# Attention and mixture: the mixture's products as single float32 matmuls instead of three rounded ones

## The chip, the cores and the metric

The kernel runs on one core of a Trainium2 chip. The metric is the device time of one execution in microseconds, and the median of the runs counts. Engines are named as in the profile: PE multiplies matrices (PEld is its loading of weights), DVE, ACT and POOL work element by element, SP issues transfers.

## What is computed

Eight batches, each of eight attention heads (576 positions, 64 wide), followed by a mixture over the joined heads (512 channels):

```python
scores = scale * np.matmul(q, k.transpose(0, 1, 3, 2))
thresh = np.max(scores, axis=-1, keepdims=True) - tau
scores = np.where(scores >= thresh, scores, -1000000000.0)
...
attn = attn / (np.sum(attn, axis=-1, keepdims=True) + 1e-09)
return np.matmul(attn, v).astype(np.float32)
...
theta = x @ w_theta
cos_t, sin_t = (np.cos(theta), np.sin(theta))
zr = x * cos_t
zi = x * sin_t
yr = np.einsum('ts,bsd->btd', w_tok_r, zr)
yi = np.einsum('ts,bsd->btd', w_tok_i, zi)
y = yr + yi
u = x + y
return (u + np.maximum(u @ w_ch, 0.0)).astype(np.float32)
```

The weights come as float64, and the kernel converts them to float32 on the chip.

## The kernel before, in words

Everything is transposed: a tile xT holds 128 channels by 576 positions. Heads go in pairs, four pairs to a batch, 32 in all. A pair has five blocks of query rows, worked off as nine "halves". One half is: scores on PE (line 278), their eviction with the row minimum on DVE (L282), exp on ACT (L299), mask and row sum on DVE (L300), transposes on PE (L326, L341) copied by ACT (L331, L344). After the second block and at the end of a pair come the values (o_ps, L361, copied to xT by L362) and the division by the row sums (normalize).

The mixture of a batch runs beside the attention of the next one. It is a generator, `moe`, that yields a cost after each piece of PE work. `fill` is called twice in each half; it adds `share` to an account and takes pieces of the mixture until the account is used up. The order of PE's instructions is the order in which the program issues them (`manual_schedule`); the other engines' order comes from priorities, where attention goes first. Attention's scores run three halves ahead (`AHEAD`). The last batch's mixture has no attention beside it.

The mixture has three stages with matmuls, in the order of `ORDER`:

- angle: th = w_theta times x, for four blocks m of 128 channels, two halves of 288 positions, four blocks to sum over (`product`, L405). th is evicted by ACT (m under 2) or DVE (L446), reduced to a fraction of a turn on DVE (km, L453, and L454, L463), and ACT takes sine and cosine (L471, L472). POOL multiplies them by x (L483), DVE in the last batch.
- token: z is transposed on PE in nine blocks (L495), evicted, and multiplied by the token weights, nine blocks to sum over (L512). The sum is added to xT in place (L515), which makes it u.
- channel: w_ch times u (`product` again), evicted with the maximum and added to u in place (L560), and u goes out by DMA (L565).

A product of two float32 matrices is made of three matmuls on rounded halves: high times high, low times high, high times low. So every operand is split: `split` copies it to a rounded type (float32r) for the high half and subtracts that for the low half. x is split when the batch's attention is done (split_x: ACT and POOL, the last chunk on DVE); z when it is evicted (zh on ACT, L497, zl on DVE, L498); u after the token stage (split_u: DVE and POOL). The token weights stay in SBUF as wt_h and wt_l. The halves of w_theta and w_ch are written to DRAM (wm_dram), and for each m POOL's queue loads them again (get_wm, L192).

The conversion of the weights is spread over the first halves: `fill` advances one of two streams at each call (`load_weight`; bit operations on ACT and DVE, L138 to L148). For w_theta and w_tok the two float32 parts are added on PE through the identity (w_ps, L159 and L160); for w_ch, which comes later, on DVE (L150).

Of the kernel before, what the change touches and what calls it, by code (L numbers as in the profile page):

```python
# [16 lines left out]
DRAM = bass.MemoryType.DRAM  # L17
# [16 lines left out]
LAG = 3  # L34
# [5 lines left out]
def tile_attn_moe(  # L40
# [22 lines left out]
    dram = ctx.enter_context(tc.tile_pool(name="dram", bufs=1, space=DRAM))  # L63
# [56 lines left out]
    turn = [0]  # L120

    def load_weight(src, n, on_pe=True):

        w = pool.tile([P, S], F32, tag="xh", name="w", bufs=4)[:, :n]
        if src.dtype == F32:
            nc.sync.dma_start(w, src)
            yield
            return [(slice(0, n), w)]
        turn[0] += 1
        tag, bufs = ("wm", 3) if turn[0] % 2 else ("z", 3)  # L130
        raw = pool.tile([P, S, 2], U32, tag=tag, name="wraw", bufs=bufs)[:, :n]
        nc.sync.dma_start(raw, src.bitcast(U32).rearrange("p (n t) -> p n t", t=2))
        low, high = raw[:, :, 0], raw[:, :, 1]
        bits = pool.tile([P, S], U32, tag="xh", name="bits", bufs=4)[:, :n]
        mag = pool.tile([P, S], U32, tag="xl", name="mag", bufs=4)[:, :n]
# [11 lines left out]
        nc.vector.tensor_scalar(out=mag, in0=bits, scalar1=0xFF800000, scalar2=None, op0=ALU.bitwise_and)  # L147
        nc.vector.scalar_tensor_tensor(out=w, in0=low, scalar=2.0**-52, in1=magf, op0=ALU.mult, op1=ALU.mult)  # L148
        if not on_pe:
            nc.vector.tensor_tensor(out=w, in0=w, in1=bitsf, op=ALU.add)  # L150
            yield
            return [(slice(0, n), w)]
        yield

        n2 = n if n <= 512 else n // 2
        got = []
        for c in range(0, n, n2):
            ps = ps_t.tile([P, 512], F32, tag="t", name="w_ps")[:, :n2]
            nc.tensor.matmul(ps, ident, bitsf[:, c : c + n2], start=True, stop=False)  # L159
            nc.tensor.matmul(ps, ident, w[:, c : c + n2], start=False, stop=True)  # L160
            got.append((slice(c, c + n2), ps))
        return got

    def load_wtok(c):
        got = yield from load_weight(w_tok[c * P : (c + 1) * P, :], S)
        for r, w in got:
            split(nc.scalar, nc.vector, wt_h[:, c, r], wt_l[:, c, r], w)

    def load_wm(which, src, c):
        got = yield from load_weight(src[c * P : (c + 1) * P, :], DM, which == 0)  # L170
        hi, lo = (pool.tile([P, DM], F32R, tag="zh4" if x == "whi" else "zl4", name=x, bufs=4) for x in ("whi", "wlo"))
        for r, w in got:
            split(nc.scalar, nc.vector, hi[:, r], lo[:, r], w)
        for i, t in enumerate((hi, lo)):
            nc.sync.dma_start(
                wm_dram[which, :, :, i, c, :].rearrange("m p e -> p m e"),
                t.bitcast(F32).rearrange("p (m e) -> p m e", e=P),
            )
# [10 lines left out]

    def get_wm(which, m):  # L190
        t = pool.tile([P, 2, NM, P], F32R, tag="wm", name=f"wm{which}", bufs=3)
        nc.gpsimd.dma_start(t, wm_dram[which, m].bitcast(F32R))  # L192
        return t
# [156 lines left out]
    def values(pr, g):  # L350
# [3 lines left out]
        if pr.n not in xT:  # L354
            xT[pr.n] = pool.tile([P, S], F32, tag="xT", name=f"xT{pr.n}", bufs=7)
# [33 lines left out]
    def product(wm, parts, todo, together):  # L389

        terms = ((0, 0), (1, 0), (0, 1))
        if together:

            runs = [[(h, *t, c) for t in terms[:2] for c in range(NM - 1)] for h in range(2)]
            runs += [[(h, *terms[2], c) for c in range(NM - 1)] for h in range(2)]
            runs += [[(h, *t, NM - 1) for t in terms] for h in range(2)]
        else:
            runs = [[(h, *t, c) for t in terms for c in range(NM)] for h in range(2)]
        tiles, count = {}, [0, 0]
        for run in runs:  # L400
            for n, (h, a, bb, c) in enumerate(run):
# [3 lines left out]
                nc.tensor.matmul(  # L405
                    tiles[h][:, :HS], wm[:, a, c, :], parts[c][bb][:, hs], start=(count[h] == 0), stop=(count[h] == 11)
                )
                count[h] += 1
                if count[h] == 12:
# [4 lines left out]
    def halves(which):  # L414
        hi = pool.tile([P, S], F32R, tag="xh", name=which + "h", bufs=4)
        lo = pool.tile([P, S], F32R, tag="xl", name=which + "l", bufs=4)
        return hi, lo

    parts = {}

    def split_x(b):
        parts[b] = []
        for c in range(NM):
            hi, lo = halves("x")
            split(nc.vector if c == NM - 1 else nc.scalar, nc.vector if c == NM - 1 else nc.gpsimd, hi, lo, xT[b * NP + c])
            parts[b].append((hi, lo))

    def moe(b):
        last = b == B - 1


        lo_eng = nc.vector if last else nc.gpsimd

        xs = parts.pop(b)
        zs = {}

        def angle(m):
            th = temp("th")
            wm = get_wm(0, m)
# [10 lines left out]
            yield from product(wm, xs, evict, m == 0)  # L450
# [6 lines left out]
        def sines(ms):  # L457

            todo = []
            for m in ms:  # L460
                th = zs.pop((m, "f"))
                z = pool.tile([P, 2 * S], F32, tag="z", name="z", bufs=3)
# [16 lines left out]
            for m, th, z in todo:  # L479
                x = xT[b * NP + m]  # L480
# [5 lines left out]
        def flip(m):  # L486
            z = zs.pop(m)
            out = []
            for c0, nb in ((0, 4), (4, 1), (5, 4)):
                zh = pool.tile([P, nb, P], F32R, tag=f"zh{nb}", name="zh", bufs=4 if nb == 4 else 2)  # L490
                zl = pool.tile([P, nb, P], F32R, tag=f"zl{nb}", name="zl", bufs=4 if nb == 4 else 2)
# [4 lines left out]
                tv = tp[:, : nb * P].rearrange("p (c q) -> p c q", q=P)  # L496
                nc.scalar.copy(out=zh, in_=tv)  # L497
                nc.vector.tensor_tensor(out=zl, in0=tv, in1=zh.bitcast(F32), op=ALU.subtract)  # L498
                out += [(zh[:, i], zl[:, i]) for i in range(nb)]
                yield 110 * nb  # L500
            zs[m, "T"] = out

        def token(m):
            zz = zs.pop((m, "T"))
            x = xT[b * NP + m]
            for h in range(2):
                hs = slice(h * HS, (h + 1) * HS)
                ps = ps_t.tile([P, 512], F32, tag="t", name="y_ps")
                work = [(zz[c][0], w[:, c, hs]) for c in range(NK) for w in (wt_h, wt_l)]
                work += [(zz[c][1], wt_h[:, c, hs]) for c in range(NK)]  # L510
                for n, (z, w) in enumerate(work):
                    nc.tensor.matmul(ps[:, :HS], z, w, start=(n == 0), stop=(n == len(work) - 1))  # L512
                    if n % 3 == 2:
                        yield 393
                nc.vector.tensor_tensor(out=x[:, hs], in0=ps[:, :HS], in1=x[:, hs], op=ALU.add)  # L515

        us = {}

        def split_u(c):
            hi, lo = halves("u")  # L520
            split(nc.vector, nc.vector if c == NM - 1 else nc.gpsimd, hi, lo, xT[b * NP + c])
            us[c] = (hi, lo)

        done = []
        left = ORDER.count("a")
        for what in ORDER.split():
# [3 lines left out]
            if what == "a":  # L530
                other = flip(ms[1]) if turns else iter(())
                for n, cost in enumerate(angle(m)):
                    yield cost
                    if n > 1:
# [3 lines left out]
                left -= 1  # L538
# [4 lines left out]
            else:  # L543
                other = flip(ms[1]) if turns else iter(())
                for n, cost in enumerate(token(m)):
                    yield cost
                    if n % 5 == 2:
# [3 lines left out]
                done.append(m)  # L551
            while left == 0 and done:
                split_u(done.pop(0))
        yield None
        for m in range(NM):
            wm = get_wm(1, m)
            u = xT[b * NP + m]

            def evict(ps, hs):
                nc.vector.scalar_tensor_tensor(  # L560
                    out=u[:, hs], in0=ps[:, :HS], scalar=0.0, in1=u[:, hs], op0=ALU.max, op1=ALU.add
                )

            yield from product(wm, us, evict, m == 0)
            nc.sync.dma_start(outT[b, m * P : (m + 1) * P, :], u)  # L565
# [4 lines left out]
    share = (16 * 3 * 524 + 4 * 990 + 72 * 393) / (per - 1) / 2  # L570
# [41 lines left out]
    with tc.manual_schedule(engines={nc.tensor.engine}):  # L612
# [3 lines left out]
        for t, (n, i, j) in enumerate(halfs):  # L616
# [83 lines left out]
```

## Time and profile before

| what | value |
|---|---|
| median of 3 runs | 1151.37 us (1150.37 to 1155.16) |
| span of the profiled execution | 1147.4 us |
| instructions | 21175 |
| mean granted PE clock in that execution | 0.981 |
| DMA traffic | 105.26 MB, mean 92 GB/s |

A row of the page's groups reads: line, engine, operation, written tile <- read tiles, shapes, count | busy us, mean ns of one | idle time of the engine just before them, and what ended most of it. A row of the timeline reads: start in us from the span's start, length in us, engine, line, operation, tiles, count, and in brackets the idle time before. In PE's rows the length of one matmul is longer than the distance to the next start, since matmuls are pipelined. A row of the windows gives busy us and, in brackets, the instructions of each engine in one stretch of time. A row of the waits gives who waited for whom, us in total, times, and the longest.

### The profile page before, as it was taken

The page shows a single profiled execution, that of the slowest core. Times are in us where ns is not written, and L with a number is a line of the kernel's source. Part 1 is how long each engine was busy: PE and PEld are TensorE (multiplying, and loading weights), DVE is VectorE, ACT ScalarE, POOL GpSimd, SP SyncE. Part 2 cuts the span into 40 slices and gives each one's busy share as a digit, 9 for nine tenths or more (in the row PEclk, how much of TensorE's full clock was granted, in tenths as well). Part 3 has the DMA queues.
Part 4 walks back from the last instruction along what each step waited for, and adds up shares of the span by engine and source line. Part 5 has one row for each costly group of instructions (what it writes and reads, how often), then busy time and mean ns, then how long its engine had stood idle before and what let it go on. Part 6 is the DMA issues. An engine that isn't in the chain of part 4 may idle for free.

```text
span 1147.4 us, 21175 instructions
## 1 busy us (share of the span) xinstructions
PE 1043.9 (91%) x7736; PEld 921.5 (80%) x7736; DVE 869.0 (76%) x2139; ACT 750.0 (65%) x1394; POOL 375.1 (33%) x303
## 2 busy tenths in 40 slices
PE   4888888799899998999979998999989999799998
PEld 3566687688779987898869987799878998689898
DVE  7998777987877677876787768776788678787362
ACT  6766869666676566964677666865678656774350
POOL 2203325233342243521443234422435314430210
PEclk9999999999999998999999999999999999999999
DMA  7722223255231052213432142311522133310421
GB/s 252 213 81 84 64 71 97 88 138 148 76 100 53 28 178 74 79 47 103 116 100 63 32 146 76 102 53 34 173 87 72 43 113 104 97 32 1 120 71 60
DMA packets 55176, 105.26 MB, mean 92 GB/s; under 512 B 11936, under 2 KB 20128, under 8 KB 55072
## 3 DMA queue, kind: packets, MB, share of 16 engines
q1 hardware_dynamic: 45856, 70.35, 20.9%
q0 software_dynamic: 9216, 33.56, 10.2%
q8 instruction: 61, 1.00, 0.4%
q14 instruction: 43, 0.35, 0.1%
HBM read 90.24 MB, written 13.63 MB: 91 GB/s over the span
## 4 chain that ended last, share of the span: by engine, by line
PE 64%; DVE 15%; ACT 13%; issue 4%; DMA 2%; POOL 1%; SPq 0%; ACTq 0%; POOLq 0%; DVEq 0%
PE y_ps L512 15%; PE m_ps L405 13%; PE o_ps L361 13%; PE s_ps L278 11%; PE t_ps L326 7%; DVE sc L282 3%; DVE s_sb L300 3%; DVE km L453 3%; ACT s_sb L299 3%; DMA qraw<-in_qT_dram 2%; ACT a L331 2%; PE rb_ps L377 1%; PE z_ps L495 1%; ACT z L471 1%; ACT z L472 1%
## 5 line engine op out<-in xcount | busy, mean ns | idle before, releaser
L300 DVE SCALAR_TENSOR_TENSOR s_sb<-sc,nm,s_sb 128x576 f32<-128x576 f32 x288 | 276.1, 960 | 69.4 <-ACT s_sb L299 65.5
L299 ACT ACTIVATE s_sb<-sc,nm 128x576 f32<-128x576 f32 x288 | 224.1, 778 | 110.8 <-DVE sc L282 109.9
L278 PE MATMUL s_ps<-k,qq 128*128 128x288 f32 (+1 forms) x1344 | 240.2, 307 | 53.8 <-DVE sc L282 39.8
L282 DVE TENSOR_SCALAR_CACHE_REDUCE sc<-s_ps 128x576 f32<-128x576 f32 x288 | 216.7, 753 | 67.2 <-PE s_ps L278 64.3
L278 PEld LDWEIGHTS s_ps<-k,qq 128*128 128x128 f32 x1344 | 193.8, 192 | 81.4 <-DVE sc L282 46.6
L361 PE MATMUL o_ps<-a,v 128*64 128x320 f32 (+1 forms) x1280 | 180.2, 430 | 31.2 <-DVE nm L295 27.7
L331 ACT COPY a<-t_ps 128x512 f32<-128x512 f32 x256 | 148.2, 579 | 58.2 <-PE t_ps L326 56.9
L326 PE MATMUL t_ps<-ident,s_sb 128*128 128x128 f32 x1152 | 175.4, 275 | 1.7 <-DVE zl L498 1.7
L361 PEld LDWEIGHTS o_ps<-a,v 128*64 128x64 f32 x1280 | 92.5, 143 | 97.8 <-ACT s_sb L299 30.4
L512 PE MATMUL y_ps<-wt_h,zh 128*128 128x288 f32 x576 | 165.2, 305 | 6.3 <-DVE zl L498 4.8
L512 PE MATMUL y_ps<-wt_l,zh 128*128 128x288 f32 x576 | 163.0, 301 | 0.0
L109 POOL TENSOR_TENSOR k<-kraw,k 128x576 fp32r<-128x576 f32 x62 | 90.8, 1465 | 202.4 <-ACT k L100 201.0
L228 POOL TENSOR_TENSOR qq<-qraw,qq 64x576 fp32r<-64x576 f32 x62 | 95.1, 1534 | 159.9 <-ACT qq L226 130.4
L326 PEld LDWEIGHTS t_ps<-ident,s_sb 128*128 128x128 f32 x1152 | 142.4, 142 | 3.8 <-DVE zl L498 1.9
L512 PEld LDWEIGHTS y_ps<-wt_h,zh 128*128 128x128 f32 x576 | 108.6, 188 | 8.1 <-DVE zl L498 6.2
L512 PEld LDWEIGHTS y_ps<-wt_l,zh 128*128 128x128 f32 x576 | 108.6, 189 | 0.0
L512 PE MATMUL y_ps<-wt_h,zl 128*128 128x288 f32 x576 | 103.6, 306 | 0.0
L192 POOL DMA_DIRECT2D wm<-wm_dram x64 | 36.4, 570 | 171.0 <-PE m_ps L405 142.6
L405 PE MATMUL m_ps<-xh,wm 128*128 128x288 f32 x512 | 91.5, 305 | 0.3 <-ACT xh L100 0.3
L483 POOL TENSOR_TENSOR z<-z,xT 128x576 f32<-128x576 f32 x56 | 80.0, 1457 | 31.5 <-ACT z L471 31.4
L109 POOL TENSOR_TENSOR ul<-xT,uh 128x576 fp32r<-128x576 f32 x24 | 34.7, 1448 | 169.8 <-DVE uh L104 169.8
L405 PE MATMUL m_ps<-uh,wm 128*128 128x288 f32 x512 | 84.0, 299 | 0.0
(85 smaller groups left out, 1641.9 us busy)
## 6 DMA issues: line engine op xcount, KB each, us to landing
wm<-wm_dram POOLq DMA_DIRECT2D x64, 512.0 KB, 4.0
qraw<-in_qT_dram SPq DMA_DIRECT2D x128, 144.0 KB, 2.9
kraw<-in_kT_dram SPq DMA_DIRECT2D x128, 144.0 KB, 2.9
out_dram<-xT SPq DMA_DIRECT2D x32, 288.0 KB, 2.2
v<-in_vp_dram SPq DMA_DIRECT2D x32, 256.0 KB, 2.7
wraw<-in_w_tok_dram SPq DMA_DIRECT2D x9, 576.0 KB, 5.0
wraw<-in_w_theta_dram SPq DMA_DIRECT2D x4, 512.0 KB, 4.4
wm_dram<-whi SPq DMA_DIRECT2D x8, 256.0 KB, 2.3
```

The costliest lines, as they stand in the source:

```text
L109: eng_lo.tensor_tensor(out=lo, in0=src, in1=hi.bitcast(F32), op=ALU.subtract)
L228: eng.tensor_tensor(out=qq[64:128], in0=raw[64:128], in1=qq[64:128].bitcast(F32), op=ALU.subtract)
L278: nc.tensor.matmul(ps[:, h, d0:d1], st, kk, start=(x == 0), stop=(x == len(todo) - 1))
L282: nc.vector.tensor_scalar(out=sc.rearrange("p (a b) -> p a b", a=2), in0=ps[:, :, :HS], scalar1=-1.0, scalar2=None, op0=ALU.mult, op1=ALU.min,
L299: nc.scalar.activation(out=e, in_=u.ps[j], func=AF.Exp, bias=nm[:, j : j + 1], scale=-1.0)
L300: nc.vector.scalar_tensor_tensor(out=e, in0=u.ps[j], scalar=nm[:, 2 + j : 3 + j], in1=e, op0=ALU.is_le, op1=ALU.mult, accum_out=u.pr.rows[ ...
L326: nc.tensor.transpose(out=tp[:, c * P : (c + 1) * P], in_=u.sf[:, k0 + c * P : k0 + (c + 1) * P], identity=ident)
L331: nc.scalar.copy(out=t.a[:, :, j, q0 : q0 + P], in_=tp.rearrange("p (c q) -> p c q", c=4))
L361: nc.tensor.matmul(o[64 * j : 64 * j + 64, :w], st, mv, start=(c == 0), stop=(c == 4))
L405: nc.tensor.matmul(tiles[h][:, :HS], wm[:, a, c, :], parts[c][bb][:, hs], start=(count[h] == 0), stop=(count[h] == 11))
L483: lo_eng.tensor_tensor(out=zi, in0=zi, in1=x, op=ALU.mult)
L512: nc.tensor.matmul(ps[:, :HS], z, w, start=(n == 0), stop=(n == len(work) - 1))
```

## The change

Each product of the mixture becomes one matmul on the float32 tiles themselves. The split of x, z and u goes: z is evicted by one ACT copy per transposed group into one tile zt. The converted weights stay in SBUF as float32 (wt for the token weights, wm for the two others), without the split, without the trip through DRAM and without POOL's loads. The output goes to a new tile `out` from the four buffers of the tag t576, which the raw q and k, th, km and rb use too, rather than in place. The conversion has buffers of its own (wbits, wmag, wlow; the tag z has four buffers instead of three), xT has nine instead of seven. The costs in the mixture's account, and with them `share`, are new.

```diff
-    wt_h = const.tile([P, NK, S], F32R, name="wt_h")
-    wt_l = const.tile([P, NK, S], F32R, name="wt_l")
-    wm_dram = dram.tile([2, NM, P, 2, NM, P], F32, name="wm_dram")
+    wt = const.tile([P, NK, S], F32, name="wt")
+    wm = [const.tile([P, NM, DM], F32, name=f"wm{i}") for i in range(2)]
...
             nc.tensor.matmul(ps, ident, bitsf[:, c : c + n2], start=True, stop=False)
             nc.tensor.matmul(ps, ident, w[:, c : c + n2], start=False, stop=True)
-            got.append((slice(c, c + n2), ps))
-        return got
+            nc.scalar.copy(out=out[:, c : c + n2], in_=ps)
...
-        got = yield from load_weight(src[c * P : (c + 1) * P, :], DM, which == 0)
-        hi, lo = (pool.tile([P, DM], F32R, tag="zh4" if x == "whi" else "zl4", name=x, bufs=4) for x in ("whi", "wlo"))
-        for r, w in got:
-            split(nc.scalar, nc.vector, hi[:, r], lo[:, r], w)
-        for i, t in enumerate((hi, lo)):
-            nc.sync.dma_start(
...
+        yield from load_weight(src[c * P : (c + 1) * P, :], wm[which][:, c], which == 0)
...
-            runs = [[(h, *t, c) for t in terms for c in range(NM)] for h in range(2)]
+            runs = [[(h, c) for c in range(NM)] for h in range(2)]
...
                 nc.tensor.matmul(
-                    tiles[h][:, :HS], wm[:, a, c, :], parts[c][bb][:, hs], start=(count[h] == 0), stop=(count[h] == 11)
+                    tiles[h][:, :HS],
+                    w[:, c, m * P : (m + 1) * P],
+                    xs[c][:, hs],
+                    start=(count[h] == 0),
+                    stop=(count[h] == NM - 1),
                 )
...
-                if n == len(run) - 1 or n % 4 == 3 and len(run) == 12:
-                    yield 131 * (len(run) if len(run) < 12 else 4)
+                if n == len(run) - 1 or n % 2 == 1:
+                    yield 242 * (n % 2 + 1)
...
-        xs = parts.pop(b)
+        xs = [xT[b * NP + c] for c in range(NM)]
...
+            zt = pool.tile([P, NK, P], F32, tag="zt", name="zt", bufs=3)
...
-                nc.scalar.copy(out=zh, in_=tv)
-                nc.vector.tensor_tensor(out=zl, in0=tv, in1=zh.bitcast(F32), op=ALU.subtract)
-                out += [(zh[:, i], zl[:, i]) for i in range(nb)]
+                nc.scalar.copy(out=zt[:, c0 : c0 + nb], in_=tp[:, : nb * P].rearrange("p (c q) -> p c q", q=P))
...
-                work = [(zz[c][0], w[:, c, hs]) for c in range(NK) for w in (wt_h, wt_l)]
-                work += [(zz[c][1], wt_h[:, c, hs]) for c in range(NK)]
-                for n, (z, w) in enumerate(work):
-                    nc.tensor.matmul(ps[:, :HS], z, w, start=(n == 0), stop=(n == len(work) - 1))
-                    if n % 3 == 2:
-                        yield 393
+                for c in range(NK):
+                    nc.tensor.matmul(ps[:, :HS], zt[:, c], wt[:, c, hs], start=(c == 0), stop=(c == NK - 1))
+                    if c % 2 == 1 or c == NK - 1:
+                        yield 242 * (1 + c % 2)
...
-            wm = get_wm(1, m)
-            u = xT[b * NP + m]
+            out = temp("out")
...
-                    out=u[:, hs], in0=ps[:, :HS], scalar=0.0, in1=u[:, hs], op0=ALU.max, op1=ALU.add
+                    out=out[:, hs], in0=ps[:, :HS], scalar=0.0, in1=xs[m][:, hs], op0=ALU.max, op1=ALU.add
...
-            nc.sync.dma_start(outT[b, m * P : (m + 1) * P, :], u)
+            nc.sync.dma_start(outT[b, m * P : (m + 1) * P, :], out)
...
-    share = (16 * 3 * 524 + 4 * 990 + 72 * 393) / (per - 1) / 2
+    share = (64 * 242 + 4 * 990 + 72 * 242) / (per - 1) / 2
```

More of the change, by code (lines that the diff above doesn't have):

```diff
@@ L16 @@
 PSUM = bass.MemoryType.PSUM
-DRAM = bass.MemoryType.DRAM
 MAGIC = 12582912.0
@@ L118, in after, with load_weight @@
         return ins
-    turn = [0]
-    def load_weight(src, n, on_pe=True):
-        w = pool.tile([P, S], F32, tag="xh", name="w", bufs=4)[:, :n]
+    def load_weight(src, out, on_pe=True):
+        n = out.shape[-1]
         if src.dtype == F32:
-            nc.sync.dma_start(w, src)
+            nc.sync.dma_start(out, src)
             yield
[L128 to L131, printed above, removed]
+            return
+        raw = pool.tile([P, S, 2], U32, tag="z", name="wraw", bufs=4)[:, :n]
         nc.sync.dma_start(raw, src.bitcast(U32).rearrange("p (n t) -> p n t", t=2))
         low, high = raw[:, :, 0], raw[:, :, 1]
-        bits = pool.tile([P, S], U32, tag="xh", name="bits", bufs=4)[:, :n]
-        mag = pool.tile([P, S], U32, tag="xl", name="mag", bufs=4)[:, :n]
+        bits = pool.tile([P, S], U32, tag="wbits", name="bits", bufs=2)[:, :n]
+        mag = pool.tile([P, S], U32, tag="wmag", name="mag", bufs=2)[:, :n]
         magf, bitsf = mag.bitcast(F32), bits.bitcast(F32)
@@ L147, in load_weight @@
         nc.vector.tensor_scalar(out=mag, in0=bits, scalar1=0xFF800000, scalar2=None, op0=ALU.bitwise_and)
+        w = out if not on_pe else pool.tile([P, S], F32, tag="wlow", name="w", bufs=2)[:, :n]
         nc.vector.scalar_tensor_tensor(out=w, in0=low, scalar=2.0**-52, in1=magf, op0=ALU.mult, op1=ALU.mult)
         if not on_pe:
-            nc.vector.tensor_tensor(out=w, in0=w, in1=bitsf, op=ALU.add)
+            nc.vector.tensor_tensor(out=out, in0=w, in1=bitsf, op=ALU.add)
             yield
-            return [(slice(0, n), w)]
+            return
         yield
         n2 = n if n <= 512 else n // 2
-        got = []
         for c in range(0, n, n2):
@@ L160, in load_weight @@
             nc.tensor.matmul(ps, ident, w[:, c : c + n2], start=False, stop=True)
-            got.append((slice(c, c + n2), ps))
-        return got
+            nc.scalar.copy(out=out[:, c : c + n2], in_=ps)
     def load_wtok(c):
-        got = yield from load_weight(w_tok[c * P : (c + 1) * P, :], S)
-        for r, w in got:
-            split(nc.scalar, nc.vector, wt_h[:, c, r], wt_l[:, c, r], w)
+        yield from load_weight(w_tok[c * P : (c + 1) * P, :], wt[:, c])
     def load_wm(which, src, c):
-        got = yield from load_weight(src[c * P : (c + 1) * P, :], DM, which == 0)
-        hi, lo = (pool.tile([P, DM], F32R, tag="zh4" if x == "whi" else "zl4", name=x, bufs=4) for x in ("whi", "wlo"))
-        for r, w in got:
-            split(nc.scalar, nc.vector, hi[:, r], lo[:, r], w)
-        for i, t in enumerate((hi, lo)):
-            nc.sync.dma_start(
-                wm_dram[which, :, :, i, c, :].rearrange("m p e -> p m e"),
-                t.bitcast(F32).rearrange("p (m e) -> p m e", e=P),
-            )
+        yield from load_weight(src[c * P : (c + 1) * P, :], wm[which][:, c], which == 0)
     def all_loads(todo):
@@ L386, in normalize, with product @@
             nc.vector.tensor_tensor(out=x[r, 512:S], in0=x[r, 512:S], in1=tl[r, 64 * j : 64 * j + 64], op=ALU.mult)
-    def product(wm, parts, todo, together):
-        terms = ((0, 0), (1, 0), (0, 1))
+    def product(w, m, xs, todo, together):
         if together:
-            runs = [[(h, *t, c) for t in terms[:2] for c in range(NM - 1)] for h in range(2)]
-            runs += [[(h, *terms[2], c) for c in range(NM - 1)] for h in range(2)]
-            runs += [[(h, *t, NM - 1) for t in terms] for h in range(2)]
+            runs = [[(h, c) for c in range(NM - 1)] for h in range(2)]
+            runs += [[(h, NM - 1)] for h in range(2)]
         else:
-            runs = [[(h, *t, c) for t in terms for c in range(NM)] for h in range(2)]
+            runs = [[(h, c) for c in range(NM)] for h in range(2)]
         tiles, count = {}, [0, 0]
         for run in runs:
-            for n, (h, a, bb, c) in enumerate(run):
+            for n, (h, c) in enumerate(run):
                 hs = slice(h * HS, (h + 1) * HS)
@@ L405, in product @@
                 nc.tensor.matmul(
-                    tiles[h][:, :HS], wm[:, a, c, :], parts[c][bb][:, hs], start=(count[h] == 0), stop=(count[h] == 11)
+                    tiles[h][:, :HS],
[3 more added lines that the diff above has]
+                    stop=(count[h] == NM - 1),
                 )
                 count[h] += 1
-                if count[h] == 12:
+                if count[h] == NM:
                     todo(tiles[h], hs)
-                if n == len(run) - 1 or n % 4 == 3 and len(run) == 12:
-                    yield 131 * (len(run) if len(run) < 12 else 4)
[L414 to L426, printed above, removed]
+                if n == len(run) - 1 or n % 2 == 1:
+                    yield 242 * (n % 2 + 1)
     def moe(b):
@@ L448, in evict @@
                     )
-            yield from product(wm, xs, evict, m == 0)
+            yield from product(wm[0], m, xs, evict, m == 0)
             km = temp("km")
```

40 lines of the change are left out of this document (9 added, 31 removed).

## The prediction

> **What bounds the kernel now.** I read the page first: busy times, then the chain of work that ended last.
>
> ```profile
> span 1147.4 us, 21175 instructions
> PE 1043.9 (91%) x7736; PEld 921.5 (80%) x7736; DVE 869.0 (76%) x2139; ACT 750.0 (65%) x1394; POOL 375.1 (33%) x303
> PE 64%; DVE 15%; ACT 13%; issue 4%; DMA 2%; POOL 1%; SPq 0%; ACTq 0%; POOLq 0%; DVEq 0%
> ```
>
> PE is busy 91% of the span and carries 64% of the chain. What PE gains or loses in matmuls moves the end, except where PE stands idle now and can fill the hole. The idle time is 1147.4 - 1043.9 = 103.5 us. Two more views say where it lies: the windows, and the waits of PE.
>
> ```profile
> 0.00:30.00 30.00, 13.33 (x43) 10.15 (x44) 21.38 (x51) 18.41 (x28) 6.22 (x14) 1.00 0.79 257
> 30.00:65.00 35.00, 27.49 (x156) 18.55 (x154) 34.33 (x83) 23.19 (x45) 6.19 (x4) 0.98 0.70 202
> 65.00:110.00 45.00, 38.63 (x225) 29.26 (x225) 41.31 (x103) 29.59 (x60) 11.39 (x9) 0.94 0.25 71
> 110.00:250.00 140.00, 122.52 (x900) 105.93 (x900) 116.12 (x294) 105.49 (x198) 49.54 (x36) 0.98 0.32 92
> 250.00:390.00 140.00, 132.08 (x1006) 117.94 (x1003) 105.29 (x265) 93.69 (x175) 50.02 (x39) 0.98 0.30 85
> 810.00:950.00 140.00, 132.10 (x1012) 117.47 (x1011) 106.65 (x265) 96.27 (x180) 53.77 (x42) 0.99 0.32 93
> PE s_ps L278 <- DVE sc L282: 39.8, 43, 3.6
> PE o_ps L361 <- DVE nm L295: 27.7, 7, 4.5
> PE y_ps L512 <- DVE zl L498: 4.8, 6, 0.8
> PE o_ps L361 <- DVE xT L515: 3.4, 7, 0.5
> PE s_ps L278 <- DVE rows L366: 3.0, 7, 0.7
> PE m_ps L405 <- POOL xl L109: 1.5, 2, 1.0
> ```
>
> The columns of a window are PE, PEld, DVE, ACT and POOL busy, then clock and DMA. The first 110 us are DVE's (34.33 of 35, 41.31 of 45): the weights are converted there, and PE idles 30.6 us. From 250 us on a batch repeats, and PE idles 7.9 us in each 140. Nearly every wait of PE ends on DVE.
>
> **What a product costs, before and after.** A product here is one 128x128 block against 288 columns: per batch 4x2x4 = 32 in the angle stage, 4x2x9 = 72 in the token stage, 32 in the channel stage, so 136, and 1088 in 8 batches. Before, each is three rounded matmuls. A clean stretch of them in the last batch, from the timeline (start, length, engine, line):
>
> ```profile
> 1087.46 1.21 PE L405 MATMUL m_ps<-xh,wm 128*128 128x288 f32 x8
> 1088.51 0.69 PE L405 MATMUL m_ps<-xl,wm 128*128 128x288 f32 x4
> 1089.04 1.23 PE L405 MATMUL m_ps<-xh,wm 128*128 128x288 f32 x8
> ...
> 88.44 0.65 PE L160 MATMUL w_ps<-w,ident 128*128 128x288 f32 x2
> 88.92 0.60 PE L326 MATMUL t_ps<-ident,s_sb 128*128 128x128 f32 x4
> ...
> 31.68 1.02 PE L159 MATMUL w_ps<-bits,ident 128*128 128x512 f32 x2
> 32.54 1.02 PE L160 MATMUL w_ps<-w,ident 128*128 128x512 f32 x2
> ...
> L159 PE MATMUL w_ps<-bits,ident 128*128 128x288 f32 x36 | 12.6, 434 | 0.0
> ```
>
> From 1087.46 to 1089.04 are 12 matmuls in 1.58 us: 0.132 us each, start to start, and 0.395 us for three. The lengths (0.3 us) overlap and are no price; the starts are.
>
> After, each product is one float32 matmul. The trace of before has that form: lines 159 and 160 add two float32 parts of a weight through PE, a 128x128 identity against 288 or 512 float32 columns. Line 159 is run 9x2 = 18 times at 288 columns, and the last row counts 36 records: a float32 matmul is two records. Both records of one line 160 take from 88.44 to 88.92, when the transposes start: 0.48 us, 0.242 each to the next digit. At 512 columns a pair takes 0.86 us, and 0.86 x 288 / 512 = 0.484. So the cost goes by columns, with no fixed part such as an unhidden weight load. I take 0.484 us for a product: 0.089 more than the three rounded ones. Over 1088 products that is 1088 x 0.089 = 96.8 us more on PE. The lower bound comes from a stretch of line 512 between attention's steps:
>
> ```profile
> 604.21 0.30 PE L512 MATMUL y_ps<-wt_h,zh 128*128 128x288 f32 x1
> ...
> 605.15 0.30 PE L512 MATMUL y_ps<-wt_l,zh 128*128 128x288 f32 x1
> ```
>
> Seven steps in 0.94 us are 0.134 each, 0.402 for three; the difference is then 0.082, and the sum 89. I take the larger, since its stretch is the longer one.
>
> The Trainium skill speaks for the other sign: Perfetto Trace Analysis, section Engine Utilization, puts PE's output at 307.2 G elements/s, halved for FP32_LOW_HIGH. By that page a whole float32 product would be an estimated 288 x 128 / 153.6 G = 0.24 us and the change would save PE about 1088 x 0.155 = 169 us. The trace has that rate for one record, and two records per product.
>
> **What PE gets back.** Off PE the change removes work: zl (line 498), the splits of x and u, the second half of every weight's split, 64 weight loads from DRAM on POOL.
>
> ```profile
> L498 DVE TENSOR_TENSOR zl<-z_ps,zh 128x512 fp32r<-128x512 f32 (+1 forms) x96 | 52.7, 550 | 27.7 <-ACT zh L497 27.5
> L104 DVE CAST uh<-xT 128x576 fp32r<-128x576 f32 x32 | 15.8, 494 | 0.1
> L109 DVE TENSOR_TENSOR xl<-xT,xh 128x576 fp32r<-128x576 f32 x8 | 11.7, 1460 | 0.0
> L109 DVE TENSOR_TENSOR wt_l<-w_ps,wt_h 128x288 fp32r<-128x288 f32 x18 | 7.9, 446 | 0.9 <-ACT wt_h L100 0.8
> L192 POOL DMA_DIRECT2D wm<-wm_dram x64 | 36.4, 570 | 171.0 <-PE m_ps L405 142.6
> ```
>
> DVE loses over 88 us by these four rows alone. It is not the bound outside the start, so only the part of it counts that PE waits for. ACT's copies stay: zt replaces zh with the same shapes. I go stage by stage.
>
> ```profile
> 8.55 1.79 PE L278 MATMUL s_ps<-k,qq 128*128 128x288 f32 x4 [8.55 <-DVE qq L228]
> 110.00:150.00 40.00, 32.29 (x230) 24.86 (x229) 31.55 (x93) 32.64 (x65) 13.29 (x9) 0.99 0.22 60
> ```
>
> Start, to 110 us: here DVE's time is PE's. wt_l takes 7.9 us off it, and two more subtractions for w_theta some 2. Not all shows, since the conversions are paced by PE's own steps: 5 us, between 0 and 10. The first 8.55 us, before any matmul, stay.
>
> First mixture, to 250 us: PE idles 17.5, and 7.7 of it in the first 40 us, in attention alone, before the mixture begins; these are untouched. From the rest zl goes: 4 us.
>
> Each steady batch, six of them (250 to some 1085 us): 7.9 us idle, in three parts. The largest is the o_ps wait, 27.7 / 6 or so. The timeline shows its cause:
>
> ```profile
> 575.54 5.52 POOL L483 TENSOR_TENSOR z<-z,xT 128x576 f32<-128x576 f32 x4
> 575.94 5.45 DVE L453 TENSOR_SCALAR km<-th 128x576 f32<-128x576 f32 x1
> 583.25 3.99 PE L361 MATMUL o_ps<-a,v 128*64 128x320 f32 x18 [4.51 <-DVE nm L295]
> 553.85 1.40 DVE L109 TENSOR_TENSOR xl<-xT,xh 128x576 fp32r<-128x576 f32 x1
> 555.98 0.80 PE L278 MATMUL s_ps<-k,qq 128*128 128x288 f32 x4 [1.57 <-DVE sc L282]
> L453 DVE TENSOR_SCALAR km<-th 128x576 f32<-128x576 f32 x32 | 45.4, 1420 | 6.9 <-ACT th L444 6.3
> ```
>
> km takes 5.45 us beside POOL's four multiplications, against 1.42 in the mean of all 32. Behind it in DVE's queue stand the next eviction of scores and the angle's, and PE runs dry 2.8 us later (583.25 - 4.51 = 578.74). The change keeps these multiplications, km, and their order. What moves: the product ahead of this km is 8 x 0.089 = 0.7 us longer, so km comes about that much later into the same 5.5 us and waits less. I take 1 us off the stall and keep 3.5. The Trainium skill (SBUF — State Buffer, section Who interferes with whom) says that the engine that issues first holds the pair of ports for its whole instruction and the other fully blocks. By that rule km would wait for one multiplication only, and an estimated 6 x 3.5 = 21 us more would come off the sum; the trace has km wait through four.
>
> The second part is the split of x's last chunk on DVE (1.40 us) and the s_ps wait of 1.57 us behind it; the split goes, and I take 1.3 us. The third is the zl, xT and rows waits, (4.8 + 3.4 + 3.0) / 7 = 1.6 us; zl is gone, but y then waits for ACT's copy: 1.2 us. Together 3.5 a batch, 21 us in six.
>
> The last batch, from 1085 us: PE waits for the split of x on POOL (xl, 1.5 us in the waits) and a little for ACT: 2 us.
>
> Two edits cost nothing by my count. The output goes to a new buffer instead of in place: same DVE instruction, same DMA. The pacing is in new cost units, but share and costs shrink alike (0.055 of the mixture for one angle product before, 0.053 after), so the order on PE stays.
>
> **The sum.** 1147.4 + 96.8 - (5 + 4 + 21 + 2) = 1212.2 us of span. The median of the runs, 1151.37, lies 4.0 us above the profiled span: 1216 us. With 89 for the matmuls and 42 returned (the ends of each stage's part added up: 10, 6, 24, 2) it is 1198; with 97 and 15 (0, 2, 12, 1) it is 1233.
>
> **The rivals.**
> More comes back: DVE is so much lighter that the km stall falls too. Then 6 x 3.5 = 21 us more go, and a further 1.4 a batch, since the o_ps group behind that stall takes 3.99 us for 18 records where 2.91 does for 20 elsewhere:
>
> ```profile
> 92.86 2.91 PE L361 MATMUL o_ps<-a,v 128*64 128x320 f32 x20
> ```
>
> That gives 1186. For it: the stall is a matter of tenths in the meeting of two engines. Against it: the multiplications and km both stay. Chance 0.18.
>
> Less comes back, and a new wait comes: the outputs now take from the four buffers that the raw q and k, th, km and rb share. If a line-560 eviction waits there for a raw tile, DVE's queue stands, the scores' eviction with it. At 1 us for each of 32 outputs: 1216 + 32 = 1248. For it: in-order DVE is where all PE's waits end. Against: an output leaves its buffer 2.2 us after its DMA is issued, by the page's row:
>
> ```profile
> out_dram<-xT SPq DMA_DIRECT2D x32, 288.0 KB, 2.2
> ```
>
> Chance 0.12.
>
> Faster: the matmuls of the mixture aren't the two records that lines 159 and 160 show, but one. A product is then 0.242 us, PE loses 1088 x 0.153 = 166 us, and the time falls to about 985, or 1040 if waits on DVE take a third of it back. It decides where a record is under (0.395 + 32 / 1088) / 2 = 0.212 us. For it: the kernel's new cost table counts 242 for a product. Against: the same types and shapes show two records of 0.242 here. Chance 0.04. The page of the Trainium skill on Engine Utilization, cited above, would make the time this one.
>
> No change (1146 to 1157): PE would have to fill all but some 10 of its 103 idle us, the 8 before the first matmul among them. Chance 0.02.
>
> **The numbers.** The forecast, 1198 to 1233, keeps 0.64. Two runs differ by up to 0.4%, so about 0.5% can be told from no change. The range takes the forecast, the most of the case with more returned and a third of the one with a new wait: 1184 to 1238. Faster 0.04, same 0.02, slower 0.94: all other cases lie above 1165.
>
> **What would show it.** Lines 405 and 512 of before become groups with 2 x 8 x 136 = 2176 records in all, 0.242 us from start to start in the timeline: half of that count, or 0.13, and I'm wrong by sign. PE's busy share rises to 94 or 95%, DVE's falls to about 63%. The waits of PE on zl are gone, the s_ps waits fall below 30 us, and an o_ps wait of 3 to 4 us stays in each batch. If a steady batch grows by much more than 136 x 0.089 - 3.5 = 8.6 us, a new wait is the reason.

## The result and the profile after

| | before | after |
|---|---|---|
| median, us | 1151.16 (1150.37 to 1155.16) | 1228.43 (1227.88 to 1229.25) |
| span of the profiled execution, us | 1147.4 | 1227.1 |
| PE busy / idle, us | 1043.9 / 103.5 | 1141.5 / 85.6 |
| mean granted PE clock | 0.981 | 0.976 |

The changed kernel takes 1.0663 of the time before (95% interval 1.0645 to 1.0681). It is slower, by 77.3 us where 65 were forecast. The page, cut to the counterparts of what the prediction quoted:

```profile
span 1227.1 us, 18530 instructions
PE 1141.5 (93%) x6648; PEld 884.8 (72%) x6648; DVE 761.4 (62%) x1961; ACT 740.5 (60%) x1366; POOL 261.9 (21%) x191
PE 73%; ACT 11%; DVE 10%; DMA 3%; issue 3%; SPq 0%; ACTq 0%; DVEq 0%
L468 PE MATMUL y_ps<-wt,zt 128*128 128x288 f32 x1152 | 326.5, 411 | 16.4 <-DVE xT L471 16.4
L380 PE MATMUL m_ps<-xT,wm 128*128 128x288 f32 x1024 | 281.2, 407 | 0.0
out_dram<-out SPq DMA_DIRECT2D x32, 288.0 KB, 2.1
```

The two groups of products have 1152 + 1024 = 2176 records, two for each of the 1088. Their pace, from the timeline of PE in the last batch:

```profile
1184.60 3.08 PE L468 MATMUL y_ps<-wt,zt 128*128 128x288 f32 x12
1187.51 0.60 PE L456 MATMUL z_ps<-ident,z 128*128 128x128 f32 x4
```

Twelve records take from 1184.60 to the next start, 2.91 us: 0.2425 each. That is the 0.242 of the forecast.

DVE lost 107.6 us of work and POOL 113, and PE's idle time fell by only 17.9 us (103.5 to 85.6). The windows, columns as before, say where it did not fall:

```profile
0.00:30.00 30.00, 10.20 (x36) 7.73 (x37) 19.24 (x43) 16.07 (x24) 5.64 (x14) 1.00 0.76 217
30.00:65.00 35.00, 28.75 (x155) 18.89 (x153) 31.76 (x75) 23.49 (x46) 6.34 (x4) 0.95 0.41 125
65.00:110.00 45.00, 40.17 (x244) 31.18 (x244) 38.51 (x97) 31.28 (x65) 6.11 (x5) 0.96 0.27 75
250.00:390.00 140.00, 133.81 (x795) 103.98 (x794) 85.66 (x226) 86.21 (x159) 32.90 (x23) 0.98 0.18 52
810.00:950.00 140.00, 133.43 (x795) 103.96 (x792) 86.40 (x227) 87.51 (x161) 34.52 (x24) 0.98 0.18 52
```

In the first 110 us PE idles 110 - 79.1 = 30.9 us, as before (30.6), although DVE is lighter there by 7.5. In the two steady windows shown, 7.9 us idle in 140 have become 6.2 and 6.6, where the forecast had 7.9 - 3.5 = 4.4. Which waits are left, by the waits of PE:

```profile
PE s_ps L255 <- DVE sc L259: 35.7, 35, 4.7
PE y_ps L468 <- DVE xT L471: 16.4, 7, 2.9
...
PE o_ps L338 <- DVE th L409: 7.8, 7, 1.1
PE o_ps L338 <- ACT zt L457: 4.8, 6, 1.1
PE o_ps L338 <- ACT a L308: 4.4, 7, 0.8
```

The o_ps wait behind km, 27.7 us in 7 before, is the 7.8 of line 409: 1.1 each. A y_ps wait has taken its place, 16.4 us in 7, with two o_ps waits behind it. The timeline of a steady batch shows both, km first:

```profile
892.33 6.46 POOL L446 TENSOR_TENSOR z<-z,xT 128x576 f32<-128x576 f32 x4 [8.56 <-ACT z L434]
892.86 1.20 DVE L416 TENSOR_SCALAR km<-th 128x576 f32<-128x576 f32 x1 [0.30 <-ACT z L435]
894.10 1.85 DVE L417 TENSOR_TENSOR th<-th,km 128x576 f32<-128x576 f32 x1
```

km meets POOL's four multiplications as before, but takes 1.20 us and not 5.45: it gets in after the first of them, and the four take 6.46 where they took 5.52. The rule of the Trainium skill that the prediction weighed (SBUF — State Buffer, Who interferes with whom: whoever issues first has the port pair for its whole instruction) fits this trace, where km waited for one multiplication, and not the one before, where it waited for all four. Now the new wait, 20 us later in the same batch:

```profile
908.91 0.78 ACT L434 ACTIVATE z<-z,small 128x576 f32<-128x576 f32 x1
...
909.59 1.24 ACT L435 ACTIVATE z<-th 128x576 f32<-128x576 f32 x2
...
911.32 1.28 ACT L276 ACT_TABLE_LOAD   x1
912.62 0.78 ACT L276 ACTIVATE s_sb<-sc,nm 128x576 f32<-128x576 f32 x1
913.41 1.28 ACT L434 ACT_TABLE_LOAD   x1
913.42 1.13 DVE L277 SCALAR_TENSOR_TENSOR s_sb<-sc,nm,s_sb 128x576 f32<-128x576 f32 x1 [2.44 <-ACT s_sb L276]
...
914.62 0.44 DVE L471 TENSOR_TENSOR xT<-y_ps,xT 128x288 f32<-128x288 f32 x1
...
915.11 1.43 PE L468 MATMUL y_ps<-wt,zt 128*128 128x288 f32 x4 [2.92 <-DVE xT L471]
...
917.43 1.12 PE L338 MATMUL o_ps<-a,v 128*64 128x256 f32 x2 [0.89 <-ACT zt L457]
...
919.15 4.18 PE L338 MATMUL o_ps<-a,v 128*64 128x256 f32 x18 [0.60 <-ACT a L308]
```

Read it from the top. Three of a pair's four sines are done when an exp of the attention (line 276) slips in ahead of the fourth: ACT loads the table for exp (1.28 us), and then the one for sin again (line 434). DVE's softmax step (L277) waits 2.44 us for that exp. Behind it in DVE's queue stands the addition that empties y's PSUM tile (L471), so PE waits 2.92 us, then 0.89 and 0.60, and then runs at half clock (granted clock 0.50): 18 matmuls in 4.18 us. In the timeline of before, too, an exp slipped in ahead of the fourth sine:

```profile
598.52 1.28 ACT L299 ACT_TABLE_LOAD   x1
...
599.81 0.78 ACT L299 ACTIVATE s_sb<-sc,nm 128x576 f32<-128x576 f32 x1
...
599.93 0.45 DVE L515 TENSOR_TENSOR xT<-y_ps,xT 128x288 f32<-128x288 f32 x1
...
600.43 2.38 PE L361 MATMUL o_ps<-a,v 128*64 128x256 f32 x20 [0.50 <-DVE xT L515]
...
600.62 1.25 DVE L300 SCALAR_TENSOR_TENSOR s_sb<-sc,nm,s_sb 128x576 f32<-128x576 f32 x1
```

There the addition (599.93) stood ahead of the softmax step (600.62) on DVE, and PE waited 0.50 us. So the split pair of tables is old; that DVE waits for it ahead of the addition is new. Both kernels load tables 47 times, 14 of them for these seven splits. The 14 in the kernel after, by line:

```profile
L276 ACT ACT_TABLE_LOAD x7 | 9.0, 1283 | 0.1
L434 ACT ACT_TABLE_LOAD x7 | 9.0, 1283 | 0.1
```

### The profile page after: what moved, and what is told of

The parts are those of the page before. It is cut to its first block, busy times and chain, and to the rows that moved or that the text cites. A ratio compares the mean times of both kernels' runs of the same rounds, so it can differ in the third digit from the quotient of the medians.

```text
span 1227.1 us, 18530 instructions
## 1 busy us (share of the span) xinstructions
PE 1141.5 (93%) x6648; PEld 884.8 (72%) x6648; DVE 761.4 (62%) x1961; ACT 740.5 (60%) x1366; POOL 261.9 (21%) x191
## 4 chain that ended last, share of the span: by engine, by line
PE 73%; ACT 11%; DVE 10%; DMA 3%; issue 3%; SPq 0%; ACTq 0%; DVEq 0%
PE y_ps L468 19%; PE m_ps L380 16%; PE o_ps L338 13%; PE s_ps L255 12%; PE t_ps L303 7%; DVE s_sb L277 2%; DMA qraw<-in_qT_dram 2%; DVE sc L259 2%; PE z_ps L456 2%; ACT s_sb L276 2%; ACT L430 1%; ACT z L434 1%; PE rb_ps L354 1%; DVE th L417 1%; ACT a L308 1%
## 5 line engine op out<-in xcount | busy, mean ns | idle before, releaser
L277 DVE SCALAR_TENSOR_TENSOR s_sb<-sc,nm,s_sb 128x576 f32<-128x576 f32 x288 | 261.7, 912 | 142.5 <-ACT s_sb L276 140.0
L468 PE MATMUL y_ps<-wt,zt 128*128 128x288 f32 x1152 | 326.5, 411 | 16.4 <-DVE xT L471 16.4
L255 PE MATMUL s_ps<-k,qq 128*128 128x288 f32 (+1 forms) x1344 | 273.1, 331 | 48.5 <-DVE sc L259 35.7
L380 PE MATMUL m_ps<-xT,wm 128*128 128x288 f32 x1024 | 281.2, 407 | 0.0
L468 PEld LDWEIGHTS y_ps<-wt,zt 128*128 128x128 f32 x1152 | 202.2, 191 | 54.4 <-DVE xT L471 19.0
L380 PEld LDWEIGHTS m_ps<-xT,wm 128*128 128x128 f32 x1024 | 181.0, 190 | 33.7
L339 ACT COPY xT<-o_ps 128x256 f32<-128x256 f32 x64 | 25.5, 398 | 114.8 <-PE o_ps L338 114.8
L457 ACT COPY zt<-z_ps 128x512 f32<-128x512 f32 (+1 forms) x96 | 45.8, 479 | 46.4 <-PE z_ps L456 46.1
L360 DVE TENSOR_TENSOR xT<-xT,rb_ps 128x512 f32<-128x512 f32 x32 | 22.0, 687 | 70.6 <-PE rl_ps L358 69.1
L272 DVE TENSOR_SCALAR nm<-nm,small 128x1 f32<-128x1 f32 x288 | 60.6, 210 | 6.1
L202 ACT ACTIVATE qraw<-qraw,small 128x576 f32<-128x576 f32 x64 | 49.6, 776 | 14.4 <-DMA qraw<-in_qT_dram 13.8
```

The costliest lines, as they stand in the source:

```text
L255: nc.tensor.matmul(ps[:, h, d0:d1], st, kk, start=(x == 0), stop=(x == len(todo) - 1))
L277: nc.vector.scalar_tensor_tensor(out=e, in0=u.ps[j], scalar=nm[:, 2 + j : 3 + j], in1=e, op0=ALU.is_le, op1=ALU.mult, accum_out=u.pr.rows[ ...
L380: nc.tensor.matmul(tiles[h][:, :HS], w[:, c, m * P : (m + 1) * P], xs[c][:, hs], start=(count[h] == 0), stop=(count[h] == NM - 1),)
L468: nc.tensor.matmul(ps[:, :HS], zt[:, c], wt[:, c, hs], start=(c == 0), stop=(c == NK - 1))
```

## The experiments

The theory: the product costs 0.089 us more because it is two slow records, and the rest of the difference is a matter of order on ACT and DVE. The rivals: the float32 operands or one of the stages cost something else; DVE's lighter load matters by itself; km's meeting with POOL decides. Ratios are to the kernel before, with the 95% interval.

**The type alone.** The changed kernel with the operands declared as rounded type, one matmul per product; the low halves' two products are left out.

```diff
-    wt = const.tile([P, NK, S], F32, name="wt")
+    wt = const.tile([P, NK, S], F32R, name="wt")
...
-            zt = pool.tile([P, NK, P], F32, tag="zt", name="zt", bufs=3)
+            zt = pool.tile([P, NK, P], F32R, tag="zt", name="zt", bufs=3)
```

(wm and xT likewise.)

> The kernel after with x, z, u and the weights kept in the rounded type, so that each product is one rounded matmul; the low halves of all operands are left out. Nothing else is changed. Theory of the price: a product falls from 0.484 to 0.132 us, 1088 x 0.352 = 383 us less on PE; PE is then no longer the bound, DVE (761 us busy) and its waits are, and the time lies at 850 to 950 us. If the type were not the price, the time would stay above 1150.

Measured: 945.85 us, 0.8206 (0.8182 to 0.8230). The page:

```profile
PE 798.9 (85%) x5560; PEld 650.0 (69%) x5560; DVE 722.8 (77%) x1961; ACT 728.9 (77%) x1366; POOL 268.1 (28%) x191
L468 PE MATMUL y_ps<-wt,zt 128*128 128x288 f32 x576 | 134.5, 325 | 12.5 <-DVE xT L471 8.3 <-ACT zt L457 4.1
L380 PE MATMUL m_ps<-xT,wm 128*128 128x288 f32 x512 | 111.8, 320 | 3.9 <-ACT th L407 3.9
```

One record per product now, 576 + 512, and PE's busy time falls by 342.6 us, 0.315 a product. The distances of the starts would give 0.484 - 0.132 = 0.352; a part of the rest is the lower clock, 0.957. The time is inside the forecast. So the price lies in the type, with the same blocks, tiles and order of the code. PE's idle time rises to 145.9 us: with PE this light the other engines show.

**The stages apart.** The token stage alone on float32 (e1; angle and channel as before), and the angle and channel stages alone (e2; token as before). The diff is cut to the tiles of the token weights; each run also has costs of its own in the mixture's account.

```diff
 e1, against before
-    wt_h = const.tile([P, NK, S], F32R, name="wt_h")
-    wt_l = const.tile([P, NK, S], F32R, name="wt_l")
+    wt = const.tile([P, NK, S], F32, name="wt")
 e2, against after
-    wt = const.tile([P, NK, S], F32, name="wt")
+    wt_h = const.tile([P, NK, S], F32R, name="wt_h")
+    wt_l = const.tile([P, NK, S], F32R, name="wt_l")
```

> The kernel before with the token stage alone as single float32 matmuls (576 of the 1088 products; z not split, wt in float32). Theory of the price (two records of 0.242 us in place of three matmuls of 0.132): 576 x 0.089 = 51 us more on PE, some 5 to 15 us of waits returned since zl is gone, so about 1193 us (1183 to 1203). Rival of the waits (the products cost PE about the same, and the change lost its time by the new wait of y_ps in the token stage, some 4 to 6 us in each of seven batches): 28 to 42 us more all the same, 1180 to 1193, but then the other stages alone must be free.

> The kernel after with the token stage as before (three rounded matmuls, zh and zl): the angle and channel stages alone are single float32 matmuls, 512 of the 1088 products. Theory of the price: 512 x 0.089 = 46 us more than before, some 5 to 15 returned by the splits of x and u, so about 1187 us (1180 to 1193); with the token stage alone it should add up to the 77 us of the whole change within 10. Rival of the waits in the token stage: nothing is lost here, 1140 to 1155 us.

Measured: e1 1203.0 us, 1.0441 (1.0410 to 1.0472); e2 1163.89 us, 1.0105 (1.0066 to 1.0144). PE's busy time grows by 57.0 and by 32.5 us, together 89.5, at granted clocks of 0.973 and 0.992. But the times do not add up: 52 and 13 us over their runs of the kernel before, 65 together against 77, so not within the 10 us that were expected. e1 lies at the upper end of its range, and e2 in neither of its two.

The traces say why. They record when the granted clock of PE is at half. If half of PE's busy time there counts as lost, the growth of the span can be parted into price, clock and idle time (an estimate). The whole change, 79.7 us of span, is 90.3 of price and 7.3 of clock, less 17.9 of idle time. The 53.5 of e1 are 49.0 of price and 8.0 of clock, less 3.5 of idle time; the 12.0 of e2 are 41.6 of price, less 9.1 of clock and 20.5 of idle time. The prices do add up (0.085 us a product in e1, 0.081 in e2); clock and waits do not. The two kernels differ in order: e1 loads tables 61 times, e2 33 times. The wait of PE that is new in e1:

```profile
PE o_ps L360 <- ACT a L330: 30.7, 7, 4.6
```

and two that are new or longer in e2:

```profile
PE s_ps L259 <- POOL k L107: 12.9, 7, 2.3
PE w_ps L154 <- DVE w L143: 8.7, 6, 3.8
```

The last row is e2's own: its conversion has one buffer for `w` (tag wlow) instead of two, and the wait was 2.9 before.

**DVE's load.** The changed kernel with the low half of z subtracted again, into a tile that nothing reads.

```diff
+                zl = pool.tile([P, nb, P], F32R, tag=f"zl{nb}", name="zl", bufs=2)
+                nc.vector.tensor_tensor(out=zl, in0=tv, in1=zt[:, c0 : c0 + nb], op=ALU.subtract)
```

> The kernel after with the subtraction of z put back on DVE (96 instructions, some 53 us); its result is used by nothing. Theory: DVE's relief returned little of what the matmuls cost, so putting half of it back costs 0 to 8 us: 1228 to 1236. Rival: the relief is what kept the loss from 97 us down to 77, and 53 of some 105 us put back cost 10 us or more: 1238 and above.

Measured: 1227.38 us, 1.0652 (1.0621 to 1.0683), DVE busy 808.8. That is the lower end of the theory's range. 47 us of DVE's work put back cost nothing, so the load of that subtraction was no price. No matmul reads its result here, so this run does not price the waits that zl set before.

**The split tables.** A first edit let the later exps wait until the pair's sines are done.

```diff
-        nc.scalar.activation(out=e, in_=u.ps[j], func=AF.Exp, bias=nm[:, j : j + 1], scale=-1.0)
+        ex = nc.scalar.activation(out=e, in_=u.ps[j], func=AF.Exp, bias=nm[:, j : j + 1], scale=-1.0)
+        if held:
+            after(ex, held[-1])
...
                 for x in ins:
                     after(exp, x)
+                held.append(exp)
```

> The kernel after; every exp of the attention that the program issues later than a pair of sine stages is ordered behind them on ACT, so that no exp comes between the sines and forces two more table loads. Theory: the wait of y_ps, 2.2 us in each of seven batches, and the two waits of o_ps behind it (1.0 and 0.6) hang on these table loads, and with them the 6.8 us at half clock that follow; 3 to 6 us less in each of seven batches, 1186 to 1207 us. Rival: the wait is POOL's and DVE's (four multiplications and the instructions beside them), and the order on ACT changes nothing: 1225 to 1231; or the held exps make attention late, above 1231.

> The kernel before with the same order on ACT. Its waits behind the table loads are the small ones (zl 0.8, xT 0.5, rows 0.4 in each batch): 5 to 12 us less, 1140 to 1146. Rival: no change.

Measured: e5 1225.77 us, 1.0629 (1.0602 to 1.0656), still 47 loads: the edit did not keep the exp out that slips in there, and so this run does not test the split. e6 1156.23 us, 1.0041 (1.0025 to 1.0057), with 33 loads: in the kernel before the split is gone, and instead of the 5 to 12 us of the theory nothing is gained. PE still waits for o_ps there, by the waits of e6:

```profile
PE o_ps L365 <- DVE th L450: 19.6, 6, 3.3
```

So fewer loads are not by themselves a gain; it depends on who waits. The second edit holds from both sides: the table for sin is loaded only behind the last exp issued before it.

```diff
+        exps.append(ex)
...
             ahead_of = after(nc.scalar.preload_act_table(AF.Sin), ab)
+            after(ahead_of, exps[-1])
```

> The kernel after with the sine table loaded only behind the exps that the program issued earlier, and later exps held behind the sines: 33 table loads in place of 47 (the earlier try to hold the exps left all 47 in). Theory: the two loads that an exp between the sines brings set the wait of y_ps (2.2 us in each of seven batches) and the two o_ps waits behind it (1.0 and 0.6), and the half clock behind these: 3 to 6 us less a batch, 1186 to 1207 us. Rival: POOL's multiplications set that wait, or another wait takes its place, as in the kernel before, where 33 loads saved nothing: 1223 to 1233.

> The kernel before with the token stage alone in float32 and the sines kept whole in the same way: 33 table loads in place of that kernel's 61. If the loads made its o_ps wait of 4.4 us and the z_ps waits (2.1) in each batch, with 6.8 us at half clock, 6 to 9 us less a batch: 1140 to 1161 us. Rival: they hang on POOL and DVE: 1198 to 1206.

Measured: after with whole sines (e9) 1197.88 us, 1.0404 (1.0386 to 1.0422); e1 with whole sines (e10) 1172.61 us, 1.0185 (1.0169 to 1.0202). Both gain 30 us against the same kernel without the edit. e9 is inside its forecast; e10 is in neither of its ranges, since 42 to 63 us were expected back. The page of e9:

```profile
span 1196.3 us, 18530 instructions
PE 1124.4 (94%) x6648; PEld 878.2 (73%) x6648; DVE 766.7 (64%) x1961; ACT 720.7 (60%) x1352; POOL 264.7 (22%) x191
```

Its groups of table loads, all but the one at the start:

```profile
L435 ACT ACT_TABLE_LOAD x16 | 20.5, 1283 | 0.3
L445 ACT ACT_TABLE_LOAD x16 | 20.5, 1283 | 0.3
```

And its waits of PE:

```profile
PE y_ps L475 <- DVE xT L478: 3.1, 7, 0.4
PE o_ps L343 <- ACT a L313: 7.5, 7, 1.1
```

The same instructions, 14 loads fewer. The y_ps wait is 3.1 where it was 16.4, and the o_ps wait for zt falls from 4.8 to 1.3; the o_ps wait for a rises from 4.4 to 7.5. Of the 30.8 us of span, 13.7 are idle time and 17.1 are busy time: the clock rises from 0.976 to 0.996. In after every steady batch has 3.4 or 6.8 us at half clock behind these waits, in e9 none has.

**km.** km formed straight from PSUM, one DVE instruction per half, in before (e7) and in after (e8); the fraction then takes one instruction with two SBUF inputs.

```diff
+                nc.vector.tensor_scalar(
+                    out=km[:, hs], in0=ps[:, :HS], scalar1=1.0 / TURN, scalar2=MAGIC, op0=ALU.mult, op1=ALU.add
+                )
...
-            nc.vector.tensor_scalar(out=km, in0=th, scalar1=MAGIC, scalar2=-MAGIC, op0=ALU.add, op1=ALU.add)
-            nc.vector.tensor_tensor(out=th, in0=th, in1=km, op=ALU.subtract)
+            nc.vector.scalar_tensor_tensor(
+                out=th, in0=km, scalar=-MAGIC, in1=th, op0=ALU.add, op1=ALU.subtract
+            )
```

> The kernel before with km computed from PSUM in two halves rather than from th in SBUF (DVE has 0.45 us more for each of 32), and the fraction by one instruction with its sign turned; the sine's scale takes the sign back. Theory: km's form from SBUF to SBUF waits through POOL's four multiplications, and the 4.5 us wait of o_ps in six batches with the half clock behind it goes: 6 x (4 to 6) = 24 to 36 us less, 1115 to 1128. Rival: whatever DVE does next is held by POOL in the same way (the next instructions read SBUF twice): no change, 1145 to 1155.

> The kernel after with the same km. Its o_ps wait behind km is only 1.1 us in each batch, so there is little to take: 1218 to 1228. If km still held DVE as in the kernel before, 1195 to 1205.

Measured: e7 1131.68 us, 0.9818 (0.9795 to 0.9842); e8 1227.88 us, 1.0644 (1.0613 to 1.0676), as after without it. e7 lies between its two ranges, 3.7 us above the theory's; e8 is inside its own. In after there was only 1.1 us a batch to get, but e8 also loads tables 61 times, 14 more than after. e7 is the fastest kernel here with the whole computation; it beats both. But it has 33 loads as well, without any edit to the order on ACT, so km with whole sines was run too, in after (e11) and in before (e12), with the edits shown.

> The kernel after with the sines whole and km from PSUM. Theory: both waits off PE's path leave little but the start: 1180 to 1200 us. If only the km form counts here, the time of the kernel after with km alone, about 1228; if only the table loads count, the time of the kernel after with the sines whole, within 4 us.

> The kernel before with the sines whole and km from PSUM, to stand beside the kernel after with both (1195.7 us): the two differ by the products and the splits alone, with the two movable waits off in both. Theory of the price: 1088 products at 82 to 89 ns are 89 to 97 us, less 5 to 12 us of waits that the splits cost, so 1105 to 1119 us. Rival: the split's work on DVE and POOL finds another wait in the kernel before, as the order of ACT alone did (1156), and the time stays at that of km alone, 1128 to 1135.

Measured: e11 1195.7 us, 1.0387 (1.0370 to 1.0404), which is e9 within the intervals, as expected if only the table loads count there. e12 1152.98 us, 1.0000 (0.9987 to 1.0013): with the same km and as few loads as e7, nothing gained, and in neither of the ranges expected. The timeline of e7 in a steady batch:

```profile
437.05 5.53 POOL L488 TENSOR_TENSOR z<-z,xT 128x576 f32<-128x576 f32 x4
438.87 4.34 DVE L457 SCALAR_TENSOR_TENSOR th<-km,th 128x576 f32<-128x576 f32 x1
439.98 0.58 ACT L333 COPY a<-t_ps 128x512 f32<-128x512 f32 x1
440.62 2.91 PE L361 MATMUL o_ps<-a,v 128*64 128x320 f32 x20 [0.35 <-ACT a L333]
```

That of e12, at the same place:

```profile
443.75 5.54 POOL L495 TENSOR_TENSOR z<-z,xT 128x576 f32<-128x576 f32 x4
445.57 4.35 DVE L462 SCALAR_TENSOR_TENSOR th<-km,th 128x576 f32<-128x576 f32 x1
446.68 1.44 ACT L301 ACTIVATE s_sb<-sc,nm 128x576 f32<-128x576 f32 x2
...
450.22 0.59 ACT L509 CAST zh<-z_ps 128x512 fp32r<-128x512 f32 x1
...
450.91 2.37 PE L366 MATMUL o_ps<-a,v 128*64 128x320 f32 x16 [3.96 <-ACT zh L509]
```

In both, the next instruction with two SBUF inputs starts 1.8 us into POOL's four multiplications and ends only behind the last of them, 4.34 and 4.35 us. So the new form of km did not take DVE's wait away, as I had thought; it moved it by one instruction. In e7 ACT copies `a` first, and PE starts o_ps after 0.35 us, beside the waiting DVE. In e12 o_ps also waits for the eviction zh, and three exps and the copies of `a` stand ahead of it on ACT: zh comes only at 450.22, and PE waits 3.96 us. Why ACT's order came out so in each was not tried.

## Why the prediction was right, and where it was off

- **The step that decides** held: two records per product, 0.2425 us each, 2176 in all; slower, and inside the range. Busy time of PE grew by 97.6 us where 96.8 was forecast. That the two nearly agree is in part luck, since 7.3 of the 97.6 are the lower clock: PE was busy for 35.2 us at half clock in before and for 49.8 in after, and half of that is taken as lost. The price alone is then an estimated 90.3 us, 0.083 a product. So the lower bound, 0.082 and 89 us, was the better one, not the 0.089 that I took.
- **The sum** missed by 1228.4 - 1216 = 12.4 us. "Returned" fell short by 14.1: 32 us forecast, 17.9 measured (idle 103.5 to 85.6). The median lies 1.3 us above the profiled span and not 4.0, which takes 2.7 back.
- **The start**: 5 us forecast, none returned in the first 110 us (30.6 and 30.9 us idle). DVE had less to do, but PE's wait for the scores' eviction there stayed (17.1 and 18.0 us, 14 times each), and where the w_ps wait of 2.9 went, two waits for k came, 4.1 together. From 110 to 250 us PE idles 15.8 us where it idled 17.5: 1.7 back, and 4 were forecast.
- **Each steady batch** grew by 10.3 us, by the starts of the o_ps waits behind km in the timelines: (1042.62 - 323.72) / 5 = 143.8 us against (981.88 - 314.40) / 5 = 133.5; 8.6 was forecast. (A batch was 133.5 us, not the 140 of the windows, so the 7.9 us idle were some 7.5 a batch.) The part for the split of x came in sum nearly as forecast: the s_ps waits for sc between 250 and 950 us fell from 10.5 to 5.4 us, 0.9 a batch where 1.3 was taken, though the wait of 1.57 itself is still 1.0. Two steps failed, in opposite directions. "I take 1 us off the stall and keep 3.5": the stall fell to 1.1, so 2.4 a batch more came back than I gave. "zl is gone, but y then waits for ACT's copy: 1.2 us" returned: in its place came the y_ps wait (16.4 / 7 = 2.3 us), the o_ps waits behind it (4.8 / 6 and 4.4 / 7, together 1.4) and the half clock. e9 prices all that at 30 us in the whole kernel.
- **The rivals.** The mechanism of the first, km's stall falling, did happen, but its time, 1186, did not come: the split tables cost 30 us, and even with whole sines the kernel takes 1197.9. Output buffers: no wait on them is among PE's or DVE's (the eviction into `out` waits for PE alone), and an output leaves its buffer 2.1 us after its issue (2.2 before). One record per product and no change: both excluded by the records and the time.
- **The marks** I named: s_ps waits below 30 us, wrong (35.7); an o_ps wait of 3 to 4 us a batch, wrong (1.1); DVE at 63%, right (62); PE at 94 or 95%, nearly (93); and "if a steady batch grows by much more than 8.6 us, a new wait is the reason": it grew by 10.3, and there is a new wait. The order on PE stayed, as the prediction had it: at each o_ps group of a steady batch the mixture stands within two products of where it stood before.

What stays open: why km gets in between POOL's multiplications in after and not before; how much of the 20.5 us that e2 waits less is its order on ACT, and how much the splits of x and u that are gone; why the same exp slips in ahead of the addition on DVE in after. The account's new costs and its pieces of two products, not one, were not varied alone; they may have a part in that order. That the order on DVE turned the old split into a wait is read from the two timelines; what was run is that without the split the 30 us go.

## What to carry to other kernels

Before three rounded matmuls become one float32 matmul, look for a float32 matmul in the trace you have, and count its records and the distance of their starts: here 2 x 0.242 us against 3 x 0.132. Work taken off engines that are not the bound returns at most the waits they cause, and those move: DVE and POOL lost over 220 us here, PE got 18. And look at the order on ACT and DVE before settling on the arithmetic: keeping one exp from between the sines was worth 30 us in one kernel and nothing in the other.

## What the runs showed of the hardware

- A table load took 1283 ns every time, and the exp behind it started 1.30 us after the load did (911.32 to 912.62). The Trainium skill (ScalarE: Activation LUTs, What ACT_TABLE_LOAD costs) gives the same 1283 ns, and about 1380 more for a drain with each switch, which no switch looked at here shows.
- A wait of PE of 2.92 us (to 915.11 in after) was enough for half clock. The granted clock is 1.00 up to 916.0, ahead of the waits of 0.89 and 0.60, and then 0.50 for 6.8 us: 18 o_ps matmuls took 4.18 us where 20 of the same shape took 2.38 in before. A longer wait need not do it: behind the 3.96 us in e12 the clock stayed at 1.00, and 16 matmuls took 2.37 us. The waits in the steady batches of after cost more in clock (17.1 us of busy time in e9's comparison) than in idle time (13.7).
- Beside POOL's run of multiplications on SBUF, a DVE instruction took 5.45 us (km, before), 4.34 (two SBUF inputs, e7), or 1.20 (km, after). In the first it waited for all four of POOL's instructions, in the second until the last of them had ended, in the third for one.
